# A state-space convolution and an MLP on one core: the second half's products summed on TensorE, first MLP blocks in halves, and a new order

## The chip, the cores and the metric

The kernel runs on one core of one Trainium2 chip. The time is device microseconds (us) of one execution; lower is better. The core has TensorE (PE, matmuls, with its weight loads shown as PEld), VectorE (DVE), ScalarE (ACT), GpSimd (POOL) and SyncE (SP, which here only issues DMA transfers). Each has a queue of its own, in program order, and waits on semaphores for the others.

## The reference

Shapes: sequence 2048, channels D = 512, states N = 128, MLP width F = 1376, bf16 inputs.

```python
def _A_ref(u, A_re, A_im, B_re, B_im, C_re, C_im, log_dt, Dskip):
    dt = jnp.exp(log_dt)[:, None]
    logdA = dt * A
    dB = dt * Bc
    P = jnp.exp(logdA[:, :, None] * l[None, None, :])
    K = jnp.einsum("dn,dnl,dn->dl", Cc, P, dB).real
    ...
    Yf = Uf * Kf
    y = irfft(Yf)[..., :L]
    return y + u * Dskip
def _B_ref(x, w1, b1, w2, b2):
    y = _layernorm(x)
    h = gelu_tanh(y @ w1 + b1)
    return h @ w2 + b2
h = u + _A_ref(_layernorm(u), A_re, ..., Dskip)
h2 = h + _B_ref(_layernorm(h), w1, b1, w2, b2)
```

So a kernel K of length 2048 is computed for each channel from complex parameters, the layer-normed sequence is convolved with it causally through Fourier transforms, and a layer-normed MLP follows, both with a residual.

## The kernel before

Everything lives in one arena of on-chip memory (`ar` in the profile) and four accumulator slots in PSUM (`ps_64` to `ps_67` in lists of the order, `ps` in the profile). The stages:

1. Parameters come in and are transposed on PE (L785, L812); exponentials of multiples of dt x A on ACT (L795, L798, L1016), Sin of angles built by PE matmuls (L1068, evaluated at L1072 on ACT), and products of both on DVE (L1039, L1079 to L1088). L1080 multiplies a sine table by -1 (the "sign pass", eight times). These make the factors of K, "the chain products".
2. K itself: 1024 small PE matmuls (L1113, L1114), evicted at L563 (ACT) or L565 (DVE); rows are carried between partitions by DMA (L1134).
3. Spectra: "xspec" (L969) and "fstage" (L989) transform sequence and K in two stages, "kspec" (L1157) is the first stage for K. K's first stage goes to DRAM and comes back in another layout (tensors `AK_d_68` to `AK_d_71`, L575): `AK_d_69` and `AK_d_68` belong to the first pair of channel groups, `AK_d_70` and `AK_d_71` to the second.
4. `inverse(b, c, ...)`: products of spectra on DVE or POOL (L1205), the sum over pairs (L1210), the inverse transform on PE (L1221) and its eviction, in two steps for each half b of the sequence and each channel group c. b = 0 has one pair, b = 1 two. After two steps `turn` sends the result through a DMA transpose (L1227). The program calls "z" what these transposes read; the first four belong to b = 0 and the fourth of them closes it.
5. "Lead" and "tail" (L1283, L1287, L1318, L1324) add the skip term and the residual and take layer-norm statistics; L1338 (DVE) or L1340 (ACT) applies them (y2), L1348 transposes on PE, two evictions fill `ybuf`, the MLP's input for 512 tokens.
6. The MLP, for four blocks of 512 tokens: w1 (L1369, 11 chunks of F with four matmuls each), GELU on ACT (L1371), w2 (L1391), residual on DVE (L1393), output by DMA.

In the products of b = 1, for which the diff has the variable name `terms`, the four terms of a complex inverse were joined to two on DVE: two operations on 128x512 (L1213) subtract and add the parts of neighbouring columns, and PE then contracts two terms with the tables TP[0] and TP[2]. For b = 0 PE contracts four terms, with TP[0], TP[1] and TP[2].

**What sets the order.** The program first records some 970 operations, each with the engines it may run on. The table ORDER lists them by number in the order of issue; a negative number takes the second engine of the two that the operation allows. `Sched.run` walks the table with estimated costs to hand out PSUM slots and to put in dummy matmuls (L1485) where it expects PE to wait. The hardware queues then follow the table. So ORDER alone decides which engine evicts what and what stands ahead of what; estimated costs change only the slots and the number of dummies.

## Time and profile before

| | us |
|---|---|
| three runs | 241.02, 240.29, 240.02 (median 240.29) |
| the profiled execution | 238.53 |
| its span, first to last instruction | 236.8 |
| chain: K matmuls done and evicted | 102.47 |
| chain: fourth transpose issued | 135.40 |
| chain: first MLP matmul | 150.00 |
| chain: last addition | 233.30 |

The granted TensorE clock was 0.99 of full speed over the span. A row of the chain of waits has start, length and what ran; "issue" is time in which nothing shown was waited for. In the groups, "x16 | 6.5, 416 | 0.2" means 16 instructions, 6.5 us busy, 416 ns each, 0.2 us idle ahead of them. In the timeline the bracket at the end gives the idle time ahead of the row and what ended it. Durations of neighbouring operations on one engine overlap by some tens of ns there.

### The profile page before, as it was taken

Reading aid. Unit: us, or ns where it says so; the run is one execution under the profiler, and the core shown is the slowest. Engines: PE = TensorE matmul, PEld = TensorE weight load, DVE = VectorE, ACT = ScalarE, POOL = GpSimd, SP = SyncE. Lnnn points to the kernel's source line nnn. Section 1 sums busy time; section 2 is a strip of 40 time slices with the busy share of each in tenths; the row PEclk is TensorE's granted clock in tenths of the full one; section 3 lists DMA queues with packets and bytes.
Section 4 is the critical chain, followed back from the end, with each engine's and each line's share of the span. In section 5 each row is a group of like instructions: output and inputs, shape, how many; then the busy total and the mean of one; then the engine's idle time right before and its main releaser. Section 6 shows DMA issues by size and latency. Waiting matters only on the chain.

```text
span 236.8 us, 7706 instructions
## 1 busy us (share of the span) xinstructions
PE 203.2 (86%) x3285; PEld 114.0 (48%) x3285; DVE 176.7 (75%) x323; ACT 172.2 (73%) x210; POOL 46.0 (19%) x224
## 2 busy tenths in 40 slices
PE   3219686768999999998979888999999999999994
PEld 2203432324875387865657544544444444444443
DVE  3999997999999975678979999988954757222022
ACT  5999999899899996696979959989456305604700
POOL 5945760000000140319400001520000101000000
PEclk9999999997999999999999999999999999999998
DMA  5692210200000549534897797470654051421212
GB/s 172 145 202 60 60 36 0 48 2 3 6 3 10 136 126 278 200 93 143 250 233 160 174 220 202 112 178 24 121 110 83 0 111 44 91 55 48 51 33 55
DMA packets 42293, 24.15 MB, mean 102 GB/s; under 512 B 25810, under 2 KB 39604, under 8 KB 42260
## 3 DMA queue, kind: packets, MB, share of 16 engines
q1 hardware_dynamic: 41810, 23.34, 41.2%
q8 instruction: 25, 0.41, 0.7%
q10 hardware_dynamic: 450, 0.33, 0.6%
q14 instruction: 8, 0.07, 0.1%
HBM read 9.90 MB, written 6.29 MB: 68 GB/s over the span
## 4 chain that ended last, share of the span: by engine, by line
PE 53%; ACT 24%; DMA 8%; DVE 7%; issue 5%; SPq 1%; POOL 1%; DVEq 0%; ACTq 0%; POOLq 0%
PE ps L1369 16%; PE ps L1391 13%; ACT ar L798 6%; ACT ar L563 6%; PE ps L1114 4%; PE ps L1113 4%; ACT ar L1072 4%; ACT ar L1016 4%; DMA ar<-ar 4%; PE ps L1068 3%; PE ps L969 3%; DMA ar<-AK_d 3%; PE ps L989 2%; ACT ar L647 2%; PE ps L1157 2%
## 5 line engine op out<-in xcount | busy, mean ns | idle before, releaser
L563 ACT CAST ar<-ps 128x1024 bf16<-128x1024 f32 (+4 forms) x72 | 65.1, 970 | 16.7 <-PE ps L1287 2.8
L1371 ACT ACTIVATE ar<-ps,ar 128x512 bf16<-128x512 f32 (+1 forms) x44 | 28.8, 688 | 30.9 <-PE ps L1369 29.7
L1369 PE MATMUL ps<-ar 128*128 128x512 bf16 (+1 forms) x176 | 40.2, 379 | 0.3 <-ACT ar L563 0.3
L1391 PE MATMUL ps<-ar 128*128 128x512 bf16 (+3 forms) x187 | 39.9, 367 | 0.0
L1072 ACT ACTIVATE ar<-ps 128x1024 bf16<-128x1024 int16 x36 | 34.7, 1049 | 1.9 <-PE ps L1068 1.6
L1393 DVE TENSOR_TENSOR ar<-ps,ar 128x512 bf16<-128x512 f32 (+1 forms) x17 | 11.2, 658 | 28.9 <-PE ps L1391 24.2
L565 DVE CAST ar<-ps 128x1024 bf16<-128x1024 f32 (+1 forms) x20 | 23.3, 1185 | 8.8 <-PE ps L1114 3.7
L1205 DVE TENSOR_TENSOR ar<-ar 128x2048 bf16<-128x2048 bf16 x21 | 25.2, 1220 | 3.6 <-PE ps L1221 3.3
L1391 PEld LDWEIGHTS <-ar 128*128 128x128 bf16 (+1 forms) x187 | 17.9, 98 | 19.8 <-issue 0.4
L1369 PEld LDWEIGHTS <-ar 128*128 128x128 bf16 (+1 forms) x176 | 17.3, 100 | 20.6 <-issue 1.1
L1068 PE MATMUL ps<-ar 128*32 128x512 f16 (+1 forms) x368 | 21.8, 346 | 5.6 <-ACT ar L1072 5.6
L1485 PE MATMUL ps<-ar 128*128 128x512 bf16 x57 | 15.7, 412 | 9.3 <-DMA ar<-in_A_u_dram 7.2
L1114 PE MATMUL ps<-ar 128*20 128x33 bf16 x512 | 20.9, 249 | 1.2 <-issue 1.2
L1113 PE MATMUL ps<-ar 128*20 128x33 bf16 x512 | 20.7, 248 | 0.5 <-issue 0.4
L925 POOL TENSOR_TENSOR ar<-ar 128x4 f32<-128x4 f32 (+1 forms) x5 | 5.7, 1148 | 77.8 <-DVE ar L614 51.5
L1113 PEld LDWEIGHTS <-ar 128*20 128x20 bf16 x512 | 18.5, 124 | 2.2 <-issue 1.3
L989 PE MATMUL ps<-ar 128*32 128x256 bf16 (+1 forms) x384 | 18.9, 310 | 0.6 <-DMA ar<-AK_d 0.3
L1114 PEld LDWEIGHTS <-ar 128*20 128x20 bf16 x512 | 18.3, 125 | 2.1 <-issue 1.7
L1068 PEld LDWEIGHTS <-ar 128*32 128x32 f16 x368 | 10.3, 101 | 15.2 <-issue 12.4
L969 PE MATMUL ps<-ar 128*32 128x512 bf16 x256 | 17.0, 380 | 0.6 <-issue 0.5
L1039 DVE TENSOR_TENSOR ar<-ar 128x2048 bf16<-128x2048 bf16 x14 | 16.5, 1212 | 0.0
L624 DVE TENSOR_TENSOR ar<-ar 128x4 f32<-128x4 f32 (+8 forms) x38 | 12.9, 352 | 3.7 <-POOL ar L693 2.8
(113 smaller groups left out, 289.4 us busy)
## 6 DMA issues: line engine op xcount, KB each, us to landing
AK_d<-ar SPq DMA_DIRECT2D x8, 512.0 KB
ar<-AK_d SPq DMA_DIRECT2D x8, 512.0 KB
ar<-in_A_u_dram SPq DMA_DIRECT2D x4, 512.0 KB
out_dram<-ar SPq DMA_DIRECT2D x30, 64.0 KB
ar<-in_B_w_dram SPq DMA_DIRECT2D x4, 344.0 KB
ar<-ar SPq DMA_DIRECT2D x20, 64.0 KB
ar<-in_B_w_dram SPq DMA_DIRECT2D x2, 640.0 KB
ar<-ar SPq DMA_DIRECT2D x8, 48.0 KB
```

The lines of the kernel that those rows point to most:

```text
L563: act.copy(out_fn(), in_fn())
L565: dve.tensor_copy(out_fn(), in_fn())
L969: pe.matmul(pst(p)[32 * cg:32 * cg + 32, 512 * z:512 * z + 512], lhsT=BD.ap()[:, 32 * f + 2 - 2 * jl:32 * f + 34 - 2 * jl], rhs=un[2 * (2 ...
L989: pe.matmul(pst(p)[64 * h + z:64 * h + z + 32, w * (k + r):w * (k + r) + w], lhsT=T.ap()[:, f, r, z:z + 32], rhs=rhs(f), start=True, stop= ...
L1068: pe.matmul(pst(p)[32 * g:32 * g + 32, 256 * j:256 * (j + n)].rearrange("p (a b) -> p a b", a=n), lhsT=W2[DELTAS.index(d)].ap(), rhs=S2[g] ...
L1072: add("ACT", c_act(1024), lambda e, o_=o_, i_=i_: act.activation(o_(), i_(), ACT.Sin, scale=SINSC), r=[p, TBL], w=[sc[cs]])
L1113: pe.matmul(o, lhsT=Ar.ap()[:, :, d], rhs=Br.ap()[:, :, d], start=True, stop=False, tile_position=(0, 32 * g))
L1114: pe.matmul(o, lhsT=Ai.ap()[:, :, d], rhs=Bi.ap()[:, :, d], start=False, stop=True, tile_position=(0, 32 * g))
L1205: (dve if e == "DVE" else gp).tensor_tensor(pieces(o).rearrange("p z (a r d) -> p a z r d", a=4, r=2), k, x, ALU.mult)
L1369: pe.matmul(pst(p)[:fs, 512 * z:512 * z + 512], lhsT=w1s[dc].ap()[:, fc * P:fc * P + fs], rhs=ybuf.ap().rearrange("p (t c) k -> p c t k", ...
L1371: add("ACT", c_act(512, 1), lambda e, p=p, z=z, fc=fc, fs=fs: act.activation(hT.ap()[:fs, fc, :], pst(p)[:fs, 512 * z:512 * z + 512], ACT. ...
L1391: pe.matmul(pst(p)[:, 512 * z + c0:512 * z + c1], lhsT=hT.ap()[:fs, fc, 128 * t:128 * t + 128], rhs=w2s[fc].ap()[:fs, c0:c1], start=(fc == ...
```

## The change

Five edits and a new table:

- `PRE` is an empty list, and the joining at L1213 and the two-term form apply only to what it lists: b = 1 now contracts four terms on PE like b = 0 (16 to 32 matmuls in each of eight steps, 16 operations of DVE gone).
- The first four chunks of the first MLP block run in halves of the tokens: four times four matmuls of 512 columns become four times eight of 256, and each half depends on its half of `ybuf` only.
- The sign pass may run on DVE or POOL (in POOL's form it is a tensor_scalar with a second multiplication by 1). The new table leaves all eight on DVE. A single other sign operation, on TP[1] (L1434), goes from DVE to POOL.
- Estimated costs (DMA issue, two PE transposes, the block of 256 PE instructions counted from 192, the wait for its refill) change. The dummy matmuls go from 57 to 60.
- ORDER is new.

In numbers of instructions, by the lists of the order, DVE goes from 323 to 312, ACT from 212 to 208, POOL from 224 to 223, SP keeps 109. Line numbers after the change are one higher up to L1366 and two higher behind it.

```diff
+PRE = []
...
 ORDER = [
-    163, -204, 0, 81, 1, 11, 12, 43, 44, 15, 132, 16, 17, 18, 2, 45, 5, 162, 3, 131, 6, 161, 66, 4, 14, 13, 46, 47, 50, 48, 62, 34, 19, 8, 60, 54, 28,
...
+    162, 0, -206, 1, 81, 43, 6, 163, 38, 12, 13, 14, 2, 11, 44, 45, 46, 15, 132, 47, 48, 3, 4, 288, 5, 141, 10, 104, 105, 16, 131, 17, 106, 18, 19,
...
-        return t0 + 3.3 + 0.4 * min(o, 5.0)
+        return t0 + 3.65 + 0.3 * min(o, 5.5)
...
-                    n1 = min(ipe, n0 - (n0 - 193) % 256 + 256)
+                    n1 = min(ipe, n0 - (n0 - 192) % 256 + 256)
...
-                add("DVE", c_dve(1024, 4), lambda e, sc=sc: dve.tensor_scalar(sc[0].ap(), sc[0].ap(), -1.0, None, ALU.mult), r=[sc[0]], w=[sc[0]])
+                add(("DVE", "POOL"), (c_dve(1024, 4), 0.92), lambda e, sc=sc: (dve if e == "DVE" else gp).tensor_scalar(sc[0].ap(), sc[0].ap(), -1.0, 1.0, ALU.mult, ALU.mult), r=[sc[0]], w=[sc[0]], hv=9)
...
-            if b:
+            if (b, c) in PRE:
                 for r, op in enumerate((ALU.subtract, ALU.add)):
                     add("DVE", c_dve(512, 2), lambda e, o=o, r=r, op=op: dve.tensor_tensor(o[0].ap()[:, :, r, :], o[0].ap()[:, :, r, :], o[1].ap()[:, :, 1 - r, :], op), r=o, w=[o[0]])
-            terms = [(0, 0, 0), (0, 1, 2)] if b else [(0, 0, 0), (1, 1, 1), (0, 1, 2), (1, 0, 2)]
+            terms = [(0, 0, 0), (0, 1, 2)] if (b, c) in PRE else [(0, 0, 0), (1, 1, 1), (0, 1, 2), (1, 0, 2)]
...
-                def fn(e, p=p, z=z, fc=fc, fs=fs):
-                    for dc in range(4):
-                        pe.matmul(pst(p)[:fs, 512 * z:512 * z + 512], lhsT=w1s[dc].ap()[:, fc * P:fc * P + fs], rhs=ybuf.ap().rearrange("p (t c) k -> p c t k", c=4)[:, dc], start=(dc == 0), stop=(dc == 3))
-                add("PE", 0.87, fn, r=[ybuf] + w1s, w=[p], new=[p] if z == 0 else [], hv=1)
+                for t0, t1 in ((0, 2), (2, 4)) if b + sb == 0 and fc < 4 else ((0, 4),):
+                    def fn(e, p=p, z=z, fc=fc, fs=fs, t0=t0, t1=t1):
+                        for dc in range(4):
+                            pe.matmul(pst(p)[:fs, 512 * z + 128 * t0:512 * z + 128 * t1], lhsT=w1s[dc].ap()[:, fc * P:fc * P + fs], rhs=ybuf.ap().rearrange("p (t c) k -> p c t k", c=4)[:, dc, t0:t1], start=(dc == 0), stop=(dc == 3))
+                    add("PE", 0.2175 * (t1 - t0), fn, r=[ybuf[4 * t0:4 * t1]] + w1s, w=[p], new=[p] if z == 0 and t0 == 0 else [], hv=1)
```

**Where instructions move.** First SP's queue from the first return of the second pair's spectra to the fifth transpose (`in_B_w` are the MLP's weights: 128x1376 a quarter of w1, 128x5x512 half of w2). Before:

```order
L575 DMA ar<-AK_d_70 128x2048
L575 DMA AK_d_71<-ar 128x8x256
L575 DMA ar<-AK_d_69 128x2048
L1227 DMA_TRANSPOSE ar<-ar 128x16x128 x3
L575 DMA ar<-in_B_w_dram 128x5x512
L1227 DMA_TRANSPOSE ar<-ar 128x16x128
L575 DMA ar<-in_B_w_dram 128x1376
L575 DMA AK_d_71<-ar 128x8x256
L575 DMA ar<-AK_d_71 128x2048 x2
L1227 DMA_TRANSPOSE ar<-ar 128x16x128 x2
```

And after the change:

```order
L576 DMA AK_d_71<-ar 128x8x256
L1228 DMA_TRANSPOSE ar<-ar 128x16x128
L576 DMA ar<-AK_d_71 128x2048
L1228 DMA_TRANSPOSE ar<-ar 128x16x128 x2
L576 DMA ar<-AK_d_71 128x2048
L1228 DMA_TRANSPOSE ar<-ar 128x16x128
L576 DMA ar<-in_B_w_dram 128x5x512
L576 DMA ar<-in_B_w_dram 128x1376 x2
L576 DMA ar<-in_B_w_dram 128x5x512
L1228 DMA_TRANSPOSE ar<-ar 128x16x128
```

The second store of AK_d_71 moved from behind the fourth transpose to ahead of the first, its two loads stand among the first four, and two halves of w2 and two quarters of w1 stand behind the fourth.

Second, ACT from the lead's evictions (128x2x384 and 128x2x128) to the first GELU. Before:

```order
L563 CAST ar<-ps_66 128x2x128 x2
L563 CAST ar<-ps_64 128x128x8
L563 CAST ar<-ps_67 128x128x8
L563 CAST ar<-ps_64 128x128x8
L1340 ACTIVATE ar<-ar 128x512 x3
L563 COPY ar<-ps_67 128x1024
L563 COPY ar<-ps_65 128x1024
L563 CAST ar<-ps_64 128x1024
L563 CAST ar<-ps_67 128x1024
L1371 ACTIVATE ar<-ps_65,ar 128x512
```

After:

```order
L564 CAST ar<-ps_64 128x2x128 x2
L564 CAST ar<-ps_67 128x1024
L558 ACT_TABLE_LOAD
L564 CAST ar<-ps_66 128x128x8
L564 CAST ar<-ps_65 128x1024
L1341 ACTIVATE ar<-ar 128x512
L564 COPY ar<-ps_66 128x1024
L564 COPY ar<-ps_65 128x1024
L1373 ACTIVATE ar<-ps_65,ar 128x512
L1373 ACTIVATE ar<-ps_66,ar 128x512
```

Two of the three y2 operations left ACT for DVE, the load of the GELU table came in (it stood some 30 rows earlier), and the spectrum evictions behind the COPYs are gone from there.

Third, ACT's first rows, up to the first group of exponentials. Before:

```order
L575 DMA ar<-in_A_log_dt_dram 1x512
L557 ACT_TABLE_LOAD
L575 DMA ar<-in_A_C_re_dram 128x512
L647 ACTIVATE ar<-ps_64 128x512
L647 ACTIVATE ar<-ar 128x512
L575 DMA ar<-in_A_B_re_dram 128x512
L795 ACTIVATE ar<-ar 128x4x128
L798 ACTIVATE ar<-ar 128x2x4x128 x9
```

After:

```order
L576 DMA ar<-in_A_log_dt_dram 1x512
L576 DMA ar<-in_A_C_re_dram 128x512
L558 ACT_TABLE_LOAD
L648 ACTIVATE ar<-ps_64 128x512
L576 DMA ar<-in_A_B_re_dram 128x512
L648 ACTIVATE ar<-ar 128x512
L796 ACTIVATE ar<-ar 128x4x128
L799 ACTIVATE ar<-ar 128x2x4x128 x3
L564 COPY ar<-ps_67 128x1024
```

The COPY of the transposed parameters C and B came to ACT from DVE, behind the third of the exponentials. On DVE the operation that forms dt x A for these exponentials (L625 after the change) stands ahead of the three small ones on integer tables that it stood behind. On PE, 16 xspec and 32 fstage matmuls that stood ahead of the last K matmul stand behind it, the last 16 kspec matmuls stand ahead of all inverses (before: behind nine of them), and all fstage matmuls stand ahead of the MLP (before: the last 32 behind its first matmuls).

14 lines of the change are left out of this document (7 added, 7 removed), and 64 rows, old and new, of the table ORDER.

## The prediction, made before the changed kernel ran

> **What bounds the kernel now.** I read the busy times first, then the chain of waits, then windows and timelines at the places that the change touches. The busy times and the chain's shares by engine:
>
> ```profile
> PE 203.2 (86%) x3285; PEld 114.0 (48%) x3285; DVE 176.7 (75%) x323; ACT 172.2 (73%) x210; POOL 46.0 (19%) x224
> PE 53%; ACT 24%; DMA 8%; DVE 7%; issue 5%; SPq 1%; POOL 1%; DVEq 0%; ACTq 0%; POOLq 0%
> ```
>
> TensorE (PE) carries half of the chain, and no engine carries the rest, so the stages have to be read one by one. Pieces of the chain in order of time (start, length, what):
>
> ```profile
> 6.07 8.52 ACT ar L798 x9
> ...
> 78.22 1.05 PE ps L969 x16
> ...
> 101.96 0.51 DVE ar L565
> ...
> 108.08 1.10 PE ps L1157 x16
> ...
> 114.65 6.03 DMA ar<-AK_d
> 120.73 1.06 PE ps L989 x32
> ...
> 128.81 4.74 ACT ar L563 x5
> ...
> 135.40 5.46 DMA ar<-ar
> ...
> 145.93 2.21 ACT ar L1340 x3
> ...
> 150.00 1.94 PE ps L1369 x8
> 151.94 0.55 PE ps L1221 x16
> ...
> 153.47 1.03 PE ps L989 x32
> ...
> 172.75 0.77 DVE ar L1213 x2
> ...
> 180.06 0.98 PE ps L1318 x8
> ...
> 195.21 9.50 PE ps L1369 x44
> ...
> 224.58 8.69 PE ps L1391 x51
> ```
>
> Five stretches: exponentials on ScalarE (ACT), of which the first nine are shown; the chain products on VectorE (DVE); PE up to the last K matmul, whose eviction is the piece at 101.96; the round trip of the spectra through memory and the inverse's evictions on ACT, up to the fourth transpose at 135.40 (I call it T4); and from 150.00 to 233.27 (the end of the last piece shown) the MLP, 83.3 us. Windows give the slack in the middle (columns: length, then busy time of PE, PEld, DVE, ACT, POOL, then clock, DMA share, GB/s):
>
> ```profile
> 60.00:80.00 20.00, 19.06 (x659) 13.22 (x647) 19.18 (x47) 18.67 (x24) 0.80 (x3) 1.00 0.08 14
> 80.00:100.00 20.00, 18.89 (x652) 14.60 (x648) 14.45 (x24) 15.14 (x17) 4.31 (x4) 1.00 0.67 211
> 100.00:120.00 20.00, 19.03 (x491) 12.52 (x483) 16.52 (x16) 17.90 (x20) 9.37 (x4) 1.00 0.59 165
> 120.00:135.00 15.00, 12.71 (x324) 8.83 (x312) 12.97 (x13) 13.29 (x15) 0.00 (x0) 1.00 0.89 170
> 135.00:150.00 15.00, 13.42 (x147) 6.80 (x148) 13.95 (x30) 11.37 (x16) 1.03 (x1) 1.00 0.93 231
> ```
>
> PE is idle 1.1 + 1.0 + 2.3 = 4.4 us from 80 to 135. In the MLP it is not: at the pitch of 9.50 / 44 = 0.216 us, the 176 mm1 matmuls take 38.0 and mm2 (the same work with 176 equivalents) about 38.1; with five inverse steps of 0.55, one spectrum step of 1.03 and two tail steps of 0.98 that is 81.8 of the 83.3. What is added there is paid, unless it fills the 1.5 that is left.
>
> **The change, part by part.**
>
> (1) *The second half's products.* The groups:
>
> ```profile
> L1213 DVE TENSOR_TENSOR ar<-ar 128x512 bf16<-128x512 bf16 x16 | 6.5, 416 | 0.2
> L1221 PE MATMUL ps<-ar 64*128 64x128 bf16 x384 | 13.4, 217 | 1.9 <-issue 1.2 <-ACT ar L563 0.5
> 116.64 1.96 PE L1221 MATMUL ps<-ar 64*128 64x128 bf16 x64
> ```
>
> DVE loses 16 x 0.416 = 6.5 us. Eight PE steps go from 16 to 32 matmuls, from 0.55 to 1.96 / 2 = 0.98 (the timeline row is two steps of 32): +0.43 each, 3.4 in all. Three of the eight stand ahead of the first MLP matmul, where dummy matmuls already fill PE, and cost nothing; without that cover they would cost 1.3. Five stand in the MLP: +2.15. The step no longer waits for the pair of DVE operations (0.77 at 172.75); the chain shows that wait fully once, the other steps have mm1 or mm2 work ahead, so I take -0.5 (bounds 0 and -1.5, all that the MLP has idle). One spectrum step (L989, 1.03 at 153.47) now stands before the MLP: -1.03. Sum in the MLP: 2.15 - 1.03 - 0.5 = **+0.6** (bounds -0.4 and +2.15, the latter if the freed DVE time buys nothing and the step is only swapped for other waiting).
>
> (2) *Halves.* The entry of the MLP, timeline rows on ACT and PE, with the prices of the operation on DVE and of the table load:
>
> ```profile
> 142.21 2.48 ACT L563 CAST ar<-ps 128x256 bf16<-128x256 f32 x4 [2.00 <-PE ps L1287]
> 145.01 1.01 ACT L563 CAST ar<-ps 128x1024 bf16<-128x1024 f32 x1 [0.32 <-PE ps L1221]
> 145.92 2.22 ACT L1340 ACTIVATE ar<-ar 128x512 bf16<-128x512 bf16 x3
> 148.05 1.91 ACT L563 COPY ar<-ps 128x1024 bf16<-128x1024 bf16 x2
> L1338 DVE TENSOR_SCALAR ar<-ar 128x512 bf16<-128x512 bf16 x8 | 2.8, 409 | 0.1
> 92.49 1.28 ACT L557 ACT_TABLE_LOAD   x1
> ```
>
> mm1 starts at 150.00, when the second COPY has ended. With halves it can start after the first, 1.91 / 2 = 0.95 earlier, and four half blocks are 16 matmuls of 256 columns. The last mm2 piece prices them: 51 matmuls in 8.69, of which 22 are halves, so (8.69 - 29 x 0.216) / 22 = 0.110 each, half of 0.216; the split itself costs nothing. Ahead of the COPY, ACT now has one L1340 instead of three (-1.4) but the table load (+1.28), which stood at 92.49 in idle time before; DVE takes two more L1338 at 0.41, beside ACT. ACT's queue from the lead's last evictions to the COPY stays about as long. Entry: **-1.0** (bounds -1.9, if ACT was not the last to be waited for and the shorter list counts, and +0.4, if PE cannot use the halves because the load shows in full: -0.95 + 1.28).
>
> [...]
>
> (3) *Up to the last K matmul.* The order puts 16 xspec (L969) and 32 fstage matmuls (L989) behind it that stood ahead: 1.05 + 1.06 = 2.1 us less on a PE that is busy 18.9 of 20 there. But they are only moved, and the order adds, ahead of T4, the kspec step of 16 (1.10 at 108.08) and 16 fstage (0.53): 1.6 more on PE, with two evictions (4.74 / 5 = 0.95 each on ACT). So T4 comes between 2.1 earlier (the moved work fits into the idle 4.4) and 1.6 later (none of it does). From 102 to 135 the chain runs over DMA and evictions, so the moved work has room; I take half of the gain, **-1.0**.
>
> (4) *The start.* Rows of the first 10 us:
>
> ```profile
> 4.01 0.75 DVE L624 TENSOR_TENSOR ar<-ar 128x17 int32<-128x17 int32 x3 [2.81 <-POOL ar L693]
> 5.44 0.63 ACT L795 ACTIVATE ar<-ar 128x512 bf16<-128x512 f32 x1 [1.54 <-DVE ar L624]
> 8.44 1.03 PE L812 MATMUL ps<-ar 128*128 128x128 bf16 x8 [3.33 <-DMA ar<-in_A_B_re_dram]
> 9.52 1.23 DVE L565 COPY ar<-ps 128x1024 bf16<-128x1024 bf16 x1 [0.25 <-PE ps L812]
> L632 ACT ACTIVATE ar<-ar 128x512 f16<-128x512 f32 x2 | 1.2, 613 | 0.0
> ```
>
> The DVE operation that ACT's first exponential waits for stood behind three that wait for GpSimd; it is first now, worth up to 1.1 (the 0.75 of the three, and part of the 2.81). Against it, the COPY moves to ACT behind three exponentials, which is at 5.44 - 1.1 + 0.63 + 3 x 8.52 / 9 = 7.8, while its transposes end at 9.47: ACT stands for up to 1.7 and then spends about 0.95 on it (as on a COPY at 148.05); the two L632 casts, 1.2, leave ACT. So between -1.1 + 0.95 - 1.2 = -1.35 (no standing) and +0.35 (all of it). The load of B that sets the 8.44 is issued at nearly the same place, so I take a value near the upper end, **-0.2**. The chain products behind it hold DVE at 19.2 of 20 and keep their number; the sign pass (8 on DVE at L1080) stays on DVE in the new order, so it gives nothing.
>
> **Sum:** +0.6 - 1.0 - 1.0 - 0.2 = -1.6 us. The profiled execution took 238.53 (span 236.8, 1.73 around it) and would take 236.9. The three timed runs have a median of 240.29, 1.76 above it; the shift carried over gives **238.7**.
>
> **The rivals.**
>
> *The second half's spectra block the transposes (slower).* SP issues in order. Before, T4 had one weight load ahead of it and the last spectra (AK_71) went out after it. Now both AK_71 stores stand ahead of the first transpose, and two AK_71 loads among the four. For it: the DMA share is 0.89 in the stretch 120 to 135. The first transpose then waits for the kspec step and its eviction, 1.1 + 0.95 = 2.05 us, if it was not already waiting for the inverse's evictions. Against: the weight load of 640 KB ahead of T4 goes behind it. Price 2.05, and the gain of 1.0 ahead of T4 is gone: -1.6 + 3.05 = +1.45, or **241.7**. From the last K eviction to T4's issue it was 135.40 - 101.96 = 33.4 us; my forecast makes it 34.5 (-2.1 and -1.0), this rival 37.6 (-2.1 and +2.05). It decides from about 37.
>
> *What is moved comes back.* The PE work put behind the last K matmul uses up its gain and T4 stays: -1.6 + 1.0 = -0.6, **239.7**. For it: 1.6 more PE work and two more evictions on engines with 2 us idle each from 120 to 135. [...]
>
> *More than I count.* Start -1.3, T4 -2.1, entry -1.5, MLP 0: -4.9, **235.4**. For it: every place has its idle time in the trace; against: all must come at once.
>
> *The change does not do what it says* holds for the sign pass alone, and moves no number.
>
> **How the numbers follow.** Forecast 0.45, its own range 237.2 to 239.8; the blocked transposes 0.28; gains handed back 0.14, of which the drain 0.03; more 0.13. A measurement of this kernel tells about 0.5% (1.2 us) from no change, so below 239.1 is faster and above 241.5 slower. Faster: 0.13 + three quarters of the forecast = 0.47; same: the rest of the forecast and what is handed back, 0.25; slower: 0.28. For 8 in 10 the range must reach both outer cases in part: 236.0 to 242.3.
>
> **What would show it.** Right: no L1213 in the second half and L1221 at 512 matmuls in about 17 us; the first L1371 (mm1's line after the change) starting before the second COPY's end; the MLP from its first matmul to the last about 84 us; T4 about 134; the first exponential near 5. Wrong: T4 past 137 with an AK transfer as releaser; ACT idle at 8 to 9.5 for PE's transposes of B; mm1 waiting for a weight DMA, since two w1 parts are issued behind T4; the table load as the releaser of the first mm1.

## The result, and the profile after

The changed kernel is slower: 242.59 us median (240.46 to 245.3, 18 runs) against 239.69 (237.55 to 242.71, 18 runs) on the same chip, a ratio of 1.0143 with a 95% interval of 1.0113 to 1.0172. The forecast was 238.7, with a range from 236.0 to 242.3. The profiled executions are 241.01 (span 239.2) and 238.53 (span 236.8), so they differ by 2.4 us where the ratio makes 3.4 (0.0143 x 239.69). One pair of executions doesn't show all of the loss, so below it is set beside the executions of other kernels that share a stage. Ratios are taken from fast runs alone, and the profiles of e4, e11, e14 and e15 are of slow ones, so no mean below has them in it.

Busy times and the chain's shares after the change:

```profile
PE 205.8 (86%) x3420; PEld 118.6 (50%) x3432; DVE 171.9 (72%) x312; ACT 170.7 (71%) x206; POOL 47.2 (20%) x223
PE 54%; DVE 17%; ACT 13%; DMA 8%; issue 5%; SPq 1%; DVEq 0%; ACTq 0%
```

PE has 2.6 us more to do and DVE 4.8 less, which is the direction that the change meant; no engine became the bound. So the stages again, along the chain of waits after the change (start, length, what):

```profile
101.40 1.54 issue
...
103.19 1.80 PE ps L990 x45
...
110.02 1.03 PE ps L1158 x16
...
115.94 6.07 DMA ar<-AK_d
122.06 1.06 PE ps L990 x32
...
125.97 2.50 PE ps L1222 x83
128.47 0.98 PE ps L970 x16
...
134.72 2.90 ACT ar L564 x3
...
148.39 0.68 DVE ar L1325
149.17 0.75 DVE ar L1339 x2
149.94 0.82 ACT ar L1341
150.76 0.91 ACT ar L564
151.72 2.81 PE ps L1371 x20
```

And the rows that close the stages: the last chain products on DVE before and after, then SP's carries of K's second set and the fourth transpose (T4), before and after:

```profile
80.12 3.42 DVE L1039 TENSOR_TENSOR ar<-ar 128x2048 bf16<-128x2048 bf16 x3
```

```profile
80.07 2.35 DVE L1040 TENSOR_TENSOR ar<-ar 128x2048 bf16<-128x2048 bf16 x2
```

```profile
102.75 3.09 SPq L1134 DMA_DIRECT2D ar<-ar  x4
...
135.40 2.68 SPq L1227 DMA_TRANSPOSE ar<-ar  x1
```

```profile
104.09 2.28 SPq L1135 DMA_DIRECT2D ar<-ar  x3
106.42 0.51 SPq L576 DMA_DIRECT2D ar<-in_B_w_dram  x1
106.98 0.73 SPq L1135 DMA_DIRECT2D ar<-ar  x1
...
138.55 1.93 SPq L1228 DMA_TRANSPOSE ar<-ar  x1
```

With the first MLP matmul at 150.00 and 151.72 that makes five stages:

| stage | before | after | difference | forecast |
|---|---|---|---|---|
| A: to the end of the last chain product | 83.54 | 82.42 | -1.1 | -0.2 |
| B: from there to the first carry of K's second set | 19.21 | 21.67 | +2.5 | -2.1 |
| C: from the carry to T4 | 32.65 | 34.46 | +1.8 | +1.1 |
| D: from T4 to the first MLP matmul | 14.60 | 13.17 | -1.4 | -1.0 |
| E: from there to the end of the span | 86.75 | 87.52 | +0.8 | +0.6 |

The forecast's -1.0 "up to the last K matmul" is split here as it was meant: 2.1 less PE work ahead of that matmul, 1.1 given back behind it. In this pair D and E came out about as forecast, C 0.7 dearer, and B is off by 4.6 us. The same stretches in the windows after the change (length, busy time of PE, PEld, DVE, ACT, POOL, clock, DMA share, GB/s):

```profile
80.00:100.00 20.00, 15.29 (x575) 12.00 (x571) 7.44 (x16) 12.52 (x14) 4.30 (x6) 1.00 0.63 198
100.00:120.00 20.00, 18.42 (x452) 11.65 (x446) 15.58 (x18) 16.72 (x18) 10.10 (x4) 1.00 0.57 152
120.00:135.00 15.00, 13.89 (x378) 9.81 (x374) 13.49 (x13) 13.65 (x16) 4.60 (x2) 1.00 1.05 222
```

From 80 to 100 PE is busy 15.29 us, with 575 matmuls; before it was 18.89 with 652. Less work was put there, and PE stands idle where it was to be done earlier. From 120 to 135 PE has 1.2 us more, ACT one instruction more, and GpSimd 4.60 where it had nothing.

### The profile page after: what moved, and what is told of

It reads as the page before. It is cut to its first block, busy times and chain, and to the rows that moved or that the text cites. A ratio compares the mean times of both kernels' runs of the same rounds, so it can differ in the third digit from the quotient of the medians.

```text
span 239.2 us, 7959 instructions
## 1 busy us (share of the span) xinstructions
PE 205.8 (86%) x3420; PEld 118.6 (50%) x3432; DVE 171.9 (72%) x312; ACT 170.7 (71%) x206; POOL 47.2 (20%) x223
## 4 chain that ended last, share of the span: by engine, by line
PE 54%; DVE 17%; ACT 13%; DMA 8%; issue 5%; SPq 1%; DVEq 0%; ACTq 0%
PE ps L1371 16%; PE ps L1393 16%; PE ps L1222 5%; ACT ar L1017 4%; PE ps L990 4%; DVE ar L1040 4%; ACT ar L564 3%; ACT ar L799 3%; DMA ar<-ar 3%; PE ps L970 3%; DMA ar<-AK_d 3%; PE ps L1115 2%; PE ps L1114 2%; DVE ar L1080 2%; PE ps L1158 2%
## 5 line engine op out<-in xcount | busy, mean ns | idle before, releaser
L564 ACT CAST ar<-ps 128x1024 bf16<-128x1024 f32 (+4 forms) x68 | 61.5, 979 | 15.4 <-PE ps L990 8.5
L1371 PE MATMUL ps<-ar 128*128 128x512 bf16 (+2 forms) x192 | 39.4, 361 | 0.5 <-ACT ar L564 0.5
L566 DVE CAST ar<-ps 128x1024 bf16<-128x1024 f32 (+1 forms) x24 | 26.9, 1131 | 15.9 <-PE ps L1115 8.2
L1371 PEld LDWEIGHTS <-ar 128*128 128x128 bf16 (+1 forms) x192 | 18.9, 100 | 19.4 <-issue 1.0
L1393 PEld LDWEIGHTS <-ar 128*128 128x128 bf16 (+1 forms) x187 | 17.9, 98 | 19.8 <-issue 0.4
L1069 PE MATMUL ps<-ar 128*32 128x256 f16 (+1 forms) x368 | 20.9, 331 | 4.2 <-ACT ar L1073 3.5
L1115 PE MATMUL ps<-ar 128*20 128x33 bf16 x512 | 19.8, 248 | 3.2 <-issue 3.2
L1114 PE MATMUL ps<-ar 128*20 128x33 bf16 x512 | 19.6, 248 | 2.2 <-issue 2.2
L1114 PEld LDWEIGHTS <-ar 128*20 128x20 bf16 x512 | 17.6, 123 | 4.8 <-issue 3.7
L1115 PEld LDWEIGHTS <-ar 128*20 128x20 bf16 x512 | 17.7, 123 | 3.1 <-issue 2.5
L990 PE MATMUL ps<-ar 128*32 128x256 bf16 (+1 forms) x384 | 17.7, 309 | 0.6 <-DMA ar<-AK_d 0.4
L1222 PE MATMUL ps<-ar 64*128 64x128 bf16 x512 | 16.6, 216 | 0.7 <-issue 0.4
L1222 PEld LDWEIGHTS <-ar 64*128 64x128 bf16 x512 | 14.4, 94 | 4.5 <-issue 2.6
L970 PE MATMUL ps<-ar 128*32 128x512 bf16 x256 | 16.4, 380 | 0.0
```

What stands on the lines that cost most here:

```text
L564: act.copy(out_fn(), in_fn())
L566: dve.tensor_copy(out_fn(), in_fn())
L990: pe.matmul(pst(p)[64 * h + z:64 * h + z + 32, w * (k + r):w * (k + r) + w], lhsT=T.ap()[:, f, r, z:z + 32], rhs=rhs(f), start=True, stop= ...
L1114: pe.matmul(o, lhsT=Ar.ap()[:, :, d], rhs=Br.ap()[:, :, d], start=True, stop=False, tile_position=(0, 32 * g))
L1115: pe.matmul(o, lhsT=Ai.ap()[:, :, d], rhs=Bi.ap()[:, :, d], start=False, stop=True, tile_position=(0, 32 * g))
L1222: pe.matmul(pst(p)[:, 512 * h + 128 * k:512 * h + 128 * k + 128], lhsT=o[z].ap()[rows, k, r, :], rhs=TP[w].ap()[rows, f0 // 2 + k, :], sta ...
```

## Experiments

Ratios are to the kernel before, measured in the same session. The stage letters are those of the table; the runs are called e1 to e18. OLD and NEW in a diff stand for the two tables.

### Each part of the change by itself

**e1: the exchange of DVE operations for PE matmuls alone**, in the old order.

```diff
+PRE = []
...
-            if b:
+            if (b, c) in PRE:
...
-            terms = [(0, 0, 0), (0, 1, 2)] if b else [(0, 0, 0), (1, 1, 1), (0, 1, 2), (1, 0, 2)]
+            terms = [(0, 0, 0), (0, 1, 2)] if (b, c) in PRE else [(0, 0, 0), (1, 1, 1), (0, 1, 2), (1, 0, 2)]
```

> The kernel before with one part of the change alone: the second half joins nothing on VectorE, TensorE sums four terms (L1213 gone, 512 matmuls at the inverse). Order otherwise as before. Theory 1 (the whole loss is this exchange): all eight steps cost 0.43 us on TensorE, +3.4 us, ratio about 1.014. Theory 2 (the exchange costs only where TensorE is the bound, in the MLP, five steps): 5 x 0.43 = 2.15 less what the shorter VectorE chain gives back (0.5 to 1.5), so +0.6 to +1.6 us, ratio 1.003 to 1.007.

Measured: 241.13, ratio 1.0114 (1.0065 to 1.0162), so 2.7 us. Stage E takes 88.6, 1.8 more than before: near the upper bound of +2.15 that the prediction gave for five longer PE steps if the freed DVE time buys nothing. Where the rest lies is not shown: B is 23.0 in this execution, but it varies by as much without any edit there (see below).

**e2: the products joined again, in the new order.**

```diff
-PRE = []
+PRE = [(1, 0), (1, 1), (1, 2), (1, 3)]
```

> The changed kernel with its products joined on VectorE again (16 operations of 0.42 us back, the second half's inverse at two terms), all else as changed. Theory 1 (the exchange is the loss): back to the time before, ratio to before about 1.000. Theory 2 (the loss lies ahead of the MLP, in the K matmuls and in the evictions ahead of the fourth transpose): about 1 us faster than the changed kernel, ratio to before about 1.010.

Measured: 247.42, ratio 1.0382 (1.033 to 1.0435); stage E 91.1, 3.6 longer than after the change. So the exchange costs in the old order and is needed in the new one, whose MLP leans on the DVE time that it frees; it can't be the cause of the loss by itself.

**e4: the changed kernel without the halves.**

```diff
-                for t0, t1 in ((0, 2), (2, 4)) if b + sb == 0 and fc < 4 else ((0, 4),):
+                for t0, t1 in ((0, 4),):
```

> The changed kernel with its first four MLP chunks whole again (176 matmuls in L1371's place instead of 192, each waiting for both evictions of the normalised tokens). If halves give what their step says, the first MLP matmul comes 0.9 us later against the fourth transpose and the time is +0.9 us, ratio to before about 1.018. If the halves give nothing because something else is waited for at the entry, ratio 1.014.

Measured: 243.98, ratio 1.0202 (1.0141 to 1.0262), 0.6% or 1.4 us above the changed kernel, though the intervals overlap. The rows show where halves gain; first the changed kernel's COPYs and first MLP matmuls, then this one's:

```profile
150.65 1.93 ACT L564 COPY ar<-ps 128x1024 bf16<-128x1024 bf16 x2
...
151.72 2.81 PE L1371 MATMUL ps<-ar 128*128 128x256 bf16 x20 [0.50 <-ACT ar L564]
```

```profile
155.09 1.93 ACT L564 COPY ar<-ps 128x1024 bf16<-128x1024 bf16 x2
...
157.06 2.75 PE L1371 MATMUL ps<-ar 128*128 128x512 bf16 x12
```

With halves PE starts 1.07 after the COPYs' start, when the first has ended; without, 1.97 after it, when both have. The 0.95 of the prediction is this 0.9. D is 14.4 here (157.06 - 142.67), 1.2 more than after the change.

**e16: halves in the old order.** The split was put on the first four chunks by number (32 matmuls of 256 columns in the trace, not the 16 that two chunks would make).

```diff
+                for t0, t1 in ((0, 2), (2, 4)) if b + sb == 0 and fc < 4 else ((0, 4),):
...
-                add("PE", 0.87, fn, r=[ybuf] + w1s, w=[p], new=[p] if z == 0 else [], hv=1)
+                    add("PE", 0.2175 * (t1 - t0), fn, r=[ybuf[4 * t0:4 * t1]] + w1s, w=[p], new=[p] if z == 0 and t0 == 0 else [], hv=1)
```

> The kernel before with the first two chunks of the first MLP block in halves of the tokens, first halves of both ahead of the second halves; nothing else. The prediction's step 2: mm1 starts 0.95 earlier, after the first COPY: 0.6 to 1.0 faster, ratio 0.996 to 0.9975. Rival (the halves only move the wait from mm1's start to the second halves, which need the second COPY at the same time as before): no change within 0.3, ratio 0.999 to 1.001.

Measured: 240.21, ratio 1.0123 (1.0078 to 1.0169). It does not test what halves at the entry give: in the old order the chunks with the lowest numbers are not the first ones that run. The first MLP row is still "128x512 x8", the 256-column matmuls come 4 us later, and their second halves hold up a GELU (stage E 88.2, 1.4 more). Even well placed there was little to gain: in the old order PE waits only 0.29 at the MLP's start, since 32 fstage matmuls fill the time ahead of it; so the 0.9 of the halves is there only in the new order, which has moved those matmuls away.

### The start

**e9: u loads behind the small restacks**, so that B_re has fewer transfers beside it. SP's queue:

```diff
-L576 DMA ar<-in_A_u_dram 64x4x1024 x3
-L576 DMA ar<-ar 64x1x512 x5
 L576 DMA ar<-in_A_u_dram 64x4x1024
+L576 DMA ar<-ar 64x1x512 x3
+L576 DMA ar<-in_A_u_dram 64x4x1024
+L576 DMA ar<-ar 64x1x512 x2
+L576 DMA ar<-in_A_u_dram 64x4x1024 x2
```

> The changed kernel; on SP the second and third load of u (512 KB each) are issued behind three and two of the small restacks that stood behind them, so that B_re's 128 KB has one load of u beside it and not three. Theory S (the start: ACT's COPY of the transposed C and B waits for B_re, which lands at its own time among the u loads; the Sin table's load on ACT came at 34.9 to 37.6 us in the runs with the changed start and at 34.54 in all three with the old one): B_re's transposes end before 8.6 us, the COPY waits for nothing, the Sin load comes at 34.9 or earlier, and the kernel is 1.4 to 1.8 us faster than the changed kernel: 240.8 to 241.2 where that has 242.6, a ratio of 1.005 to the kernel before. Rival N (the landing of B_re varies by itself, not by what is issued behind it): COPY at 9.6 to 10.5 and Sin at 36 to 37.5 again, no change. Rival L (the layer-norm of u, now later, is late for the first spectrum step): Sin at 34.9, but the first spectrum matmuls later and the first-set carries not earlier, total unchanged or slower.

Measured: 244.33, ratio 1.026 (1.0211 to 1.0309). ACT stands for 1.40 at the COPY, as in e8 (1.39):

```profile
10.03 1.01 ACT L564 COPY ar<-ps 128x1024 bf16<-128x1024 bf16 x1 [1.40 <-PE ps L813]
```

Rival N holds: the wait did not go when fewer transfers were issued beside B_re.

**e10: the COPY back on VectorE.**

```diff
-70, 71, 92, 73, 74, 62, 37, 72,
+70, -72, 92, 73, 74, 62, 37, 72,
```

> The changed kernel with one number of the order negated: the COPY of the transposed C and B runs on VectorE again, as before the change, not on ACT behind three exponentials. Theory S: ACT no longer stands for 1.0 to 1.9 us and is rid of the 1.0 of the COPY itself, so the twelve exponentials end about 2 to 3 us sooner than in the other runs of the changed order; the wait goes to VectorE, which has the chain products to do that the Sin angles need only later. The Sin load at 34.5 or earlier, 1 to 2 us off the changed kernel: ratio to the kernel before about 1.005. Rival V (VectorE is the engine that sets the end of this stage, as it is 96 per cent busy from 60 to 80 us in the kernel before): VectorE stands instead, Sin earlier on ACT, but the last chain product not earlier than 81.2 to 83 us; total unchanged within 0.5.

Measured: 243.24, ratio 1.0212 (1.0164 to 1.026). ACT no longer waits for the COPY and waits as long for DVE, five rows on:

```profile
14.48 1.23 ACT L648 ACTIVATE ar<-ar 128x512 f32<-128x512 f32 x2 [1.55 <-DVE ar L625]
```

Stage A ends at 83.40. The wait moved, as the rival said.

**e11: dt x A first, in the old kernel.** On DVE:

```diff
-L624 TENSOR_TENSOR ar<-ar 128x17 x3
 L1258 MEMSET ar 128x11
 L624 TENSOR_TENSOR ar<-ps_65,ar 128x512
+L624 TENSOR_TENSOR ar<-ar 128x17 x3
```

> The kernel before; the VectorE operation dt x A that the first exponential waits for is moved ahead of the three integer-table operations that wait for GpSimd, as the changed order does; nothing else. If the gain that the prediction saw in the start is real, the first exponential starts at about 4.4 instead of 5.44, the exponentials and the Sin load come 1.0 earlier (33.5), and the kernel is up to 1.0 us faster (ratio 0.996). Rival: the chain products on VectorE set the end of the stage, and the last one starts at 81.3 to 82.3 as before: no change within 0.3.

Measured: 238.23, ratio 0.9991 (0.9955 to 1.0027). The first exponential comes at 4.37 instead of 5.44 and the Sin table's load at 34.35 instead of 34.54: 1.07 of gain shrinks to 0.19 by then.

**e18: the old start in the changed kernel.**

```diff
-ORDER = NEW
+ORDER = OLD[:186] + [x for x in NEW if x not in OLD[:186]]
```

> The changed kernel with the old order up to the load of the Sin table on ScalarE, the new one behind it. If the new start costs 1 us by itself: Sin load at 34.5 to 34.7, last chain product's end near 83, ratio 1.009 to 1.011. Rival (the chain products on VectorE set this stage whatever ScalarE does, and the loss is behind them): Sin earlier, but no gain, ratio 1.013 to 1.016.

Measured: 242.02, ratio 1.0134 (1.009 to 1.0178). The Sin load is at 34.53, as in the old kernel, and stage A still ends at 83.73. The rival holds again. In all, the Sin load came at 34.3 to 34.7 in the kernels with the old start and at 34.9 to 37.6 in those with the new one, but no run shows the time to hang on that: an earlier Sin load gained nothing in e11 and here, and e10 moved a wait without gain. So the theory that the start makes the loss fell.

### The stretch of the K matmuls (B)

PE's pauses in that stretch, in which it waits for nothing that the profile shows, after the change and before:

```profile
92.74 0.23 PE L1114 MATMUL ps<-ar 128*20 128x33 bf16 x1 [2.20 <-issue]
97.57 0.23 PE L1115 MATMUL ps<-ar 128*20 128x33 bf16 x1 [1.66 <-issue]
102.94 0.22 PE L1115 MATMUL ps<-ar 128*20 128x33 bf16 x1 [1.54 <-issue]
```

```profile
89.26 0.25 PE L1114 MATMUL ps<-ar 128*20 128x33 bf16 x1 [0.36 <-issue]
97.26 0.25 PE L1114 MATMUL ps<-ar 128*20 128x33 bf16 x1 [0.55 <-issue]
100.99 0.25 PE L1114 MATMUL ps<-ar 128*20 128x33 bf16 x1 [0.32 <-issue]
```

Together 5.4 us of such pauses after and 1.4 before (with pauses under 0.15 us left out).

**e5 and e6: dummy matmuls put into the last K groups**, 2.2 us of PE work that nobody needs, in the changed kernel (e5) and in the old one (e6).

```diff
+                    dum = 5 if c == 3 and nb == 0 and lo == 0 else 0
...
+                        for _ in range(dum):
+                            pe.matmul(pst(p)[:, 0:512], lhsT=identb.ap(), rhs=W[0].ap().rearrange("p t q -> p (t q)"), start=True, stop=True)
```

> The changed kernel with ten dummy matmuls of 512 columns (0.216 us each, 2.2 us) put in front of two groups of K matmuls of the last channel group, five each; they write accumulators that the K matmuls overwrite. Theory of instruction delivery (TensorE stands 2.2, 1.7 and 1.5 us among the K matmuls because the next block of its instructions is not there): the dummies run in that time, the last K eviction moves by less than 0.8 us against the changed kernel (about 103.5 us), the pauses shrink by some 1.5 to 2 us in sum. Rival (TensorE is the bound by its work there, as the prediction had it): +2.2 us.

> The kernel before with the same ten dummy matmuls (2.2 us) at the same two places. There the pauses among the K matmuls sum to 1.4 us only. Theory of instruction delivery: little room, the last K eviction (101.96) moves by 0.8 to 1.8 us. Rival (work is the bound): +2.2 us, in both kernels alike.

Measured, in one run each beside 239.84 for the kernel before: 242.69 and 238.25. Stage B took 21.6 in the changed kernel with the dummies (21.67 without) and 20.1 in the old one (19.21 without); the pauses shrank from 5.4 to 3.4 and from 1.4 to 0.5. In the changed kernel 2.2 us of long matmuls cost nothing there that these single executions show, and the pauses became 2.0 shorter. That is what one sees if the pauses, and not the work, set the end; the count over more executions below says the same for the work that the change takes out.

**e15 and e17: the move alone, in the old kernel.** In e15 the edit left two evictions of moved work ahead of K's own eviction on DVE, which then came at 110.6 instead of 102, so it measured that:

```diff
-ORDER = OLD
+ORDER = OLD with xspec 495, 496 and fstage 501, 507, 513, 515, 412 behind K's last matmul 433, and fstage 509, 511 ahead of it
```

> The kernel before, products joined on VectorE; only the spectrum work is moved as in the changed order: 16 xspec and 48 fstage matmuls of 0.55 to 1.06 a step go behind the last K matmul and 16 fstage come ahead of it. The prediction's step 3 has the last K matmul up to 2.1 earlier and T4 about 1.0 to 2.1 earlier (ratio 0.993 to 0.996). Theory M: PE's end of K is set by the delivery of its instructions, so the last K matmul comes no earlier, and the moved work shows in full behind it: T4 1 to 1.9 later, ratio 1.004 to 1.008.

Measured: 244.65 to 253.24 in six runs, median 251.58, beside 238.63 for the kernel before. The same move with K's eviction first is e17:

> The kernel before with the spectrum work moved as in the changed order (16 xspec and 40 fstage matmuls behind the last K matmul, 16 fstage ahead of it), K's eviction first on VectorE. Step 3 of the prediction: the last K matmul 1 to 2 earlier after the last chain product, T4 1 to 2 earlier, ratio 0.993 to 0.997. Theory M: the way from the last chain product's end to the first carry stays at 19.2 or above (PE gets its instructions no faster), and the evictions that are moved with the work stand in ScalarE's and VectorE's queues ahead of T4: carry to T4 33.5 to 34.5 against 32 to 32.7, ratio 1.004 to 1.010.

Measured: 250.56, ratio 1.0444 (1.0383 to 1.0504). Stage A ends at 82.51, and the carry comes at 106.64: B is 24.1, not 17 to 18 as step 3 would have it. 4.7 of it are pauses, and part of the rest is a lower clock (twice 3.4 us at 0.50, see the last section). C is 39.9, since K's spectra now wait behind the moved work. Two of the pauses:

```profile
89.30 0.28 PE L1113 MATMUL ps<-ar 128*20 128x33 bf16 x4 [1.65 <-issue]
...
99.50 1.80 PE L969 MATMUL ps<-ar 128*32 128x512 bf16 x14 [2.87 <-issue]
```

Neither half of step 3 shows here. The changed order does the same move with other neighbours and loses less.

**e7 and e12: AK loads moved away.** All four loads of the first pair's spectra behind the carries (e7); and (e12, with the u loads late and the COPY on DVE) one load of AK behind the carries, another and the 96x512 weight load behind the AK_70 stores. SP's queue in the first:

```diff
-L576 DMA ar<-AK_d_69 128x2048
-L576 DMA ar<-AK_d_68 128x2048 x2
-L576 DMA ar<-AK_d_69 128x2048
 L1135 DMA ar<-ar 12x2048 x3
 L576 DMA ar<-in_B_w_dram 96x512
 L1135 DMA ar<-ar 12x2048
+L576 DMA ar<-AK_d_68 128x2048
+L576 DMA ar<-AK_d_69 128x2048
+L576 DMA ar<-AK_d_68 128x2048
+L576 DMA ar<-AK_d_69 128x2048
```

> The changed kernel with the four loads of the first pair's spectra (512 KB each, issued from 90.6 to 96.7 us, while the K matmuls run) behind the carries of the last K matmuls. Later stages wait for these loads, so the whole will be several us longer; what counts is the time of the last K eviction. Theory C (the blocks of TensorE's instructions come late because of these transfers on the same DMA engines): the pauses of 1.66 and 1.54 us at 95.9 and 101.4 fall below 0.6 and the last K eviction comes 2 to 3 us earlier than 103.5. Rival (the pauses come from too many short instructions in a row, whatever the transfers do): pauses and time as in the changed kernel within 0.5 us.

> The changed kernel with three repairs together: u loads late, the COPY on VectorE, and the loads that stood around the carries of K's second set moved behind them (one load of AK behind the carries, one load of AK and half of w2 behind the two AK_70 stores). Theory: the start gives 1.8, the carry half of w2's 0.56 and a part of PE's pauses in the stretch (5.4 to 2.4 with all four loads gone), the pauses because the loads share the DMA engines with the fetch of PE's instructions; together -2.5 to -4: 238.6 to 240, ratio 0.995 to 1.003. In the trace: Sin at 34.5 or earlier, last chain product by 81, first carry of the second set by 102.5, T4 by 137. Rival P (the pauses are of the order of PE's instructions and not of the loads): pauses stay at 5, carry at 103.5, total 240.5 to 241.

Measured: 248.84 in one run (239.84 before), and 243.86, ratio 1.0256 (1.02 to 1.0313). They shorten B to 19.2 and 19.1, with pauses of 2.4 and 3.1 and nearly the same matmuls in it (633 and 621 in place of 643); both pay more for it in C (40.8 and 36.0), because the spectra that T4 needs come late. The repairs of e12 were to bring 238.6 to 240, and didn't. In e7 the DMA engines are nearly still behind the stores of AK, and the windows show PE with and without transfers beside it (columns as above, DMA share last but one):

```profile
92.00:96.00 4.00, 1.95 (x118) 1.77 (x107) 1.98 (x10) 2.37 (x3) 1.77 (x2) 0.95 0.89 277
98.00:102.00 4.00, 4.00 (x164) 3.88 (x156) 1.60 (x2) 2.53 (x3) 0.78 (x1) 0.88 0.02 4
```

The one long pause that is left, 2.22, lies nearly all in the first of them; in the second, with a DMA share of 0.02, PE doesn't pause. So in this execution the long pause lies beside the transfers, and with the loads moved the pauses sum to 2.4 where they were 5.4. That the transfers make the pauses, by way of PE's instructions, was the theory and is not shown: in the changed kernel the pauses that end at 92.74 and 97.57 have DMA shares of 0.83 and 0.73 beside them, and the one from 101.40 to 102.94 has 0.00.

**e8: the weight load behind the fourth carry.**

```diff
-L1135 DMA ar<-ar 12x2048 x3
+L1135 DMA ar<-ar 12x2048 x4
 L576 DMA ar<-in_B_w_dram 96x512
-L1135 DMA ar<-ar 12x2048
```

> The changed kernel with the one weight load that stands between the third and the fourth carry behind the fourth. The load's issue took 0.51 us there: the last carry and the spectrum behind it (kspec at 110.02) come 0.5 us earlier. If the carries were waiting for something else, no change there.

Measured: 241.47 in one run, against 239.84; C 33.9 in place of 34.46, the 0.56 that this transfer stands between the carries. A single run can't tell that from no change.

**B over all executions.** In every execution B is PE's busy time and its pauses, and little else. By the order up to the last K matmul (means, with the range of B):

| order there | profiles | B | PE busy | pauses |
|---|---|---|---|---|
| old | before, e1, e13 (below), e16 | 21.1 (19.2 to 23.0) | 18.0 | 3.1 |
| new | after, e2, e3, e8, e9, e10, e18 | 21.5 (19.8 to 22.5) | 16.4 | 5.0 |

The new order takes 1.6 us of PE's work out of B, of the 2.1 that the prediction counted, and the pauses grow by 1.9. So the forecast gain is not there, and the 2.5 that B lost in the pair is not there either: the old kernel's profile is the one with the fewest pauses of its order (1.4, where the other three have 3.2 to 3.9).

### Behind the last K matmul (C to E)

**e13: the old order up to the last K matmul, the new one behind it.**

```diff
-ORDER = NEW
+ORDER = OLD[:475] + [x for x in NEW if x not in OLD[:475]]
```

> The changed kernel (four terms, halves) with the old order for everything up to the last K matmul and the new one for what stands behind it; so the start is the old one, and the 16 xspec and 32 fstage matmuls stand ahead of the last K matmul again. Theory M (start 1.0, the K stretch and the moved work 3 to 4): ratio to the kernel before 0.998 to 1.004; last chain product ends at 82.3 to 83.5 us, first carry of the second set by 103 (105 in an execution with long pauses of PE), the way from carry to the fourth transpose 32 to 33 against 34.1 in the changed kernel. Rival D (the loss is behind the last K matmul, in the order of the spectra and their evictions there): the way stays at 34, ratio 1.008 to 1.012. Rival E (it is in the MLP): ratio above 1.01 and the MLP 2 longer than before.

Measured: 240.57, ratio 1.0115 (1.0068 to 1.0163). Undoing all that comes ahead of the carries takes back 0.3% of 1.4%, less than the intervals tell apart, so by the medians most of the loss lies behind, as rival D had it. Its stages: C 33.8, D 12.9, E 87.8. C parts the two orders: 31.3 to 32.7 in four profiles with the old order there (before, e1, e6, e16), 33.7 to 35.5 in eight with the new one (after, e2, e5, e8, e9, e10, e13, e18), means 32.1 and 34.2. (Of the profiles that are left out of the means, e11 with the old order has 31.9, e14 with the old one 33.6 and e4 with the new one 35.5.) ACT shows why. From the carry to T4 (length, ACT's busy time and instructions, clock, DMA share, GB/s), before, after, in this run and in e3 below:

```profile
102.75:135.40 32.65, 29.06 (x31) 1.00 0.77 182
104.09:138.55 34.46, 31.76 (x35) 1.00 0.85 199
104.28:138.06 33.78, 30.79 (x34) 1.00 0.82 198
105.59:137.50 31.91, 28.18 (x30) 1.00 0.83 192
```

ACT is idle for 2.7 to 3.7 us in each of them, and C follows ACT's work. The last long rows, before and in this run:

```profile
124.28 11.09 ACT L563 CAST ar<-ps 128x1024 bf16<-128x1024 f32 x12 [1.44 <-PE ps L1221]
```

```profile
124.10 15.72 ACT L564 CAST ar<-ps 128x1024 bf16<-128x1024 f32 x17 [0.29 <-PE ps L970]
```

Twelve evictions in a row end at 135.37, and T4 follows at 135.40; now seventeen end at 139.82, and T4 comes behind one of the last of them, at 138.06. From the carry to T4 DVE evicts more too, 15 steps of 128x1024 after the change where it was 11. The additional ones are spectra: in that stretch PE runs 91 matmuls more at L970, L990 and L1158 than before, and 16 more at L1222.

**e3: T4's last two inverse steps ahead of those spectra**, with the first transpose up as well.

```diff
-416, 610, 724, 465, 601, -603, 536, 417, 603, 604, 607, 605, 726, 735, 414, 606, 608, 729, 415, 523, 539, 540, 727, 730, 731, 542, 467, 530, 543, 537,
+416, 610, 724, 465, 523, 601, -603, 536, 539, 540, 542, 543, 417, 603, 604, 607, 605, 726, 735, 414, 606, 608, 729, 415, 727, 730, 731, 467, 530, 537,
```

> The changed kernel with the last two inverse steps of the first half, and their evictions on ScalarE, moved ahead of five spectrum evictions that stood in front of them (order alone, the same work). Theory A (these five evictions of 0.95 us hold the fourth transpose, 138.55 in the changed kernel): the fourth transpose is issued near 135.5 to 136 us, the MLP begins 1.5 to 2.8 us earlier, ratio to before about 1.003 to 1.008. Theory B (the moved evictions are needed just as soon by the second half): the transpose comes earlier but the MLP does not, ratio as for the changed kernel, 1.014.

Measured: 245.54, ratio 1.029 (1.0245 to 1.0335). C falls to 31.9, as short as in the old order, with 30 instructions on ACT in place of 35: it was those evictions. But D becomes 18.8, and E is as before. The chain names the next wait, the second load of AK_71, which SP issues between the third and the fourth transpose:

```profile
135.72 1.03 ACT ar L564
136.83 6.25 DMA ar<-AK_d
143.13 0.62 PE ps L990 x16
```

The new order has all spectra of the second half ahead of the first MLP matmul on PE, so making them later only moved the wait.

**e14: the old order up to T4, the new one behind it.**

```diff
-ORDER = NEW
+ORDER = OLD[:623] + [x for x in NEW if x not in OLD[:623]]
```

> The changed kernel with the old order up to the fourth transpose; the new one, with the halves, the table load at the entry and the new MLP order, only behind it. If the loss is all ahead of T4: T4 at 135 to 136, entry 1.3 shorter (13.2 from T4 to the first mm1), MLP 0.7 longer: 0.6 faster than before, ratio 0.996 to 0.999. Rival E (four terms in the second half cost more than the 0.7 seen): ratio 1.003 or above, as in the run where the exchange stood alone in the old order (1.0114).

Measured: 247.46, ratio 1.0405 (1.034 to 1.0471). The same from the other side: with the old queue of SP the AK_71 loads come behind T4, and PE runs dummies until they land,

```profile
142.37 8.79 PE L1487 MATMUL ps<-ar 128*128 128x512 bf16 x39
```

so that the first MLP matmul is at 162.0. This way of joining the two orders doesn't give the new MLP part without paying for the second half's spectra ahead of it.

## Why the prediction was wrong

**Step (1), right.** E is 0.8 longer in the pair, +0.6 was forecast. L1222, with 512 matmuls, takes 16.6 us (forecast about 17). Run e2 shows that the freed DVE time is used, e1 that without the new order E grows by 1.8, within the bounds.

**Step (2), right.** D is 1.4 shorter in the pair, 14.5 to 13.2 over the profiles of either order, forecast -1.0, and the rows of e4 give the halves 0.9 of it. The GELU table's load is not on the chain: it runs at 146.83 for 1.28, and the next eviction starts 0.01 after it. The 0.03 that the forecast gave to a drain, time of ACT beyond the load itself, has no run behind it. Before the change a load (1.28) stands between two activations, with 0.02 idle ahead of it and 0.01 behind it:

```profile
34.28 0.24 ACT L647 ACTIVATE ar<-ar 128x8 f32<-128x8 f32 x1
34.54 1.28 ACT L557 ACT_TABLE_LOAD   x1
35.83 0.63 ACT L647 ACTIVATE ar<-ar 128x512 f32<-128x512 f32 x1
```

In e13 the load stands at 92.01 and D is 12.9, so in these profiles it costs 0.3 at most at the entry.

**Step (3) failed**, "2.1 us less on a PE that is busy 18.9 of 20 there". The number was read rightly and the conclusion was not. Work did leave the stretch (1.6 us in the means), but PE's pauses grew by 1.9, and B did not get shorter: 21.5 where it was 21.1, against a forecast of -2.1. What sets the end of these small matmuls is in large part PE's pauses (5.0 of 21.5 us in the means of the new order), and not only the time for which PE runs: with e5's 2.2 us of filler the pauses are 2.0 shorter and B is no longer. The profile shows nothing that PE waits for in them. And the profile that was read has the fewest pauses of its order, so that PE looked nearly full.

Its other half was mis-sized. "The order adds 1.6" behind the last K matmul, at worst, and half of the gain was to be left at T4, so C +1.1; C measures 1.8 more in the pair and 2.1 in the means. The PE time was counted, but of evictions only two; from the carry to T4 ACT has four instructions more and DVE four evictions more, and ACT's evictions set T4. "From 102 to 135 the chain runs over DMA and evictions, so the moved work has room" had it the wrong way round: a chain that runs over evictions has no room for more evictions.

**Step (4)** was taken at -0.2, and no run gives the start more. The wait that it named, ACT standing for B's transposes, varies between executions of the same start: nothing in the changed kernel's own profile, where the COPY runs at 8.54, and 1.0 to 2.4 in e2 to e5 and e7 to e9. E10, e11 and e18 show no gain in the time from a change there.

**The rivals.** The side that came true was that of the blocked transposes, and its time, 241.7, was near. That is luck, since its mechanism was not the one: T4 was issued 35.3 after K's eviction (138.55 - 103.29, the first row below), near the forecast's 34.5 and short of the 37 from which it decides, and of SP's waits from 112 to 140 us (total, times, longest) the transposes' are for ACT's evictions, and the one for an AK transfer is a load's:

```profile
103.29 0.50 DVE L566 CAST ar<-ps 128x330 bf16<-128x330 f32 x1 [2.85 <-PE ps L1115]
```

```profile
SPq L1228 <- ACT ar L564: 18.1, 4, 8.1
...
SPq L576 <- DMA AK_d<-ar: 0.8, 1, 0.8
```

"What is moved comes back" had the right mechanism behind the last K matmul (more evictions on engines without room) and too low a price, since it too counted on the gain ahead of that matmul and kept the rest.

**The sum.** By the means of the profiles that share a stage's order:

| stage | old | new | difference | forecast |
|---|---|---|---|---|
| A | 83.2 | 84.0 | +0.8 | -0.2 |
| B | 21.1 | 21.5 | +0.4 | -2.1 |
| C | 32.1 | 34.2 | +2.1 | +1.1 |
| D | 14.5 | 13.2 | -1.3 | -1.0 |
| E | 86.8 | 87.7 | +0.9 | +0.6 |

(A: before, e1, e6, e13, e16, e17, e18 against after, e2, e3, e5, e7, e8; B and C as above; D: before, e1, e6, e16 against after, e5, e8, e9, e10, e13, e18; E: before and e6 against those and e3.) They make 2.9 of the 3.4 us. Of the 4.5 between that and the forecast's -1.6, 2.5 are B's, and C and A have 1.0 each. A varies from 82.4 to 85.9 with the new start, and e18 with the old one gains nothing, so A's part is not shown. E13 puts 2.7 (1.6 to 3.9) behind the carries, more than the 1.7 of C, D and E here; how the loss divides to better than 1 us stays open. No version here is shown to beat the old kernel; e11 equals it.

## What to carry to other kernels

A busy engine need not be the bound of a stretch: where it runs many small instructions, count instructions and pauses too, and put filler in to see whether work there costs anything before taking work out for gain. A move out of one stage brings its evictions into the next; count them on the queue that the next stage's last wait names. And read a stage from several executions, and from several kernels that share it, before a difference of 2 us is believed.

## What the runs showed of the hardware

**PE's pauses among the small matmuls.** The page counts, after the change,

```profile
q8 instruction: 27, 0.44, 0.8%
```

27 packets of 16 KB. In the DMA view, cut into windows of 0.2 us, such packets start in the windows from 90.4, 95.2 and 100.6, and PE goes on after its pauses at 92.74, 97.57 and 102.94, each 2.1 to 2.4 us later; the packet that starts in the window from 85.2 has no such pause behind it. The view doesn't say which engine a packet is for, and the pauses are rows of "issue". That the packets bring PE's instructions and that PE waits for them is the author's inference; no run shows it. What the runs show is the pauses: in the changed kernel 2.20, 1.66 and 1.54 us while PE goes through 512 small matmuls and as many weight loads, in e17 1.65 and 2.87, and in the old kernel, with the same 512, at most 0.55.

**The clock behind stretches with pauses.** In the old kernel the granted clock is 0.50 from 54.41 to 57.82 and 1.00 from there to 235.3; in the changed kernel it is 1.00 from 20.4 to 238.8. In e1 it is 0.50 for the 3.41 us from 99.57; e17 has two such falls (a mean clock of 0.67 and 0.90 in the windows from 88 and 92, 0.95 and 0.62 in those from 96 and 100, each of 4 us). Two windows of 3.41 us in the old kernel with the exchange alone (e1), the second of them the fall, and two beside each other in the changed kernel (granted clock third from the right):

```profile
96.16:99.57 3.41, 1.50 (x67) 1.17 (x62) 2.58 (x7) 1.11 (x2) 1.43 (x2) 1.00 0.40 157
99.57:102.98 3.41, 3.41 (x68) 2.70 (x63) 0.00 (x0) 1.00 (x2) 0.00 (x0) 0.50 0.02 5
```

```profile
88.66:92.07 3.41, 1.88 (x114) 1.71 (x103) 1.39 (x9) 2.31 (x3) 1.78 (x2) 1.00 0.88 273
92.07:95.49 3.42, 2.75 (x119) 2.23 (x122) 0.61 (x2) 1.06 (x2) 1.64 (x2) 1.00 0.77 236
```

In e1 a pause of 1.91 lies whole in the first window, PE is busy for 1.50 of 3.41 there, and the clock is lower behind it. In the old kernel PE is busy for 1.60 of the 3.41 us ahead of the fall, and its longest wait there is 1.21, for ACT. In the changed kernel a pause of 2.20 (90.54 to 92.74) is split between the two windows, PE is busy for 1.88 and 2.75, and the clock stays; it also stays behind the 3.41 us that end with that pause (from 89.33), in which PE is busy for 1.21. So in these executions the length of a pause alone does not decide, and PE's busy time in the 3.41 us that end with it doesn't either; what does is not shown.
